# A fused attention, soft MoE and feed-forward kernel: six half-width phases of the feed-forward part, weight conversions over 29 steps

## The chip, the cores and the metric

The kernel runs on one NeuronCore of one Trainium2 chip. The metric is the time of one execution on the device in microseconds (us), as the median of three runs. One further execution was profiled; every row below is from it. The engines are TensorE (PE; its weight loads are PEld), VectorE (DVE), ScalarE (ACT), GpSimd (POOL) and the queue of SyncE (SP), which issues the DMAs.

## The reference, cut to what matters

Three parts follow each other: band attention with global tokens, a soft mixture of experts, and a feed-forward layer. The change is in the last.

```python
def _moe_ref(x, phi, w1, w2):          # x: 2176 tokens of 512
    ...
    return (c @ slot_out).astype(np.float32)      # c: tokens x 32 slots, slot_out: 32 x 512

def _moe2_ref(x, w_in, w_out):         # w_in 512 x 2048, w_out 2048 x 512
    h = x @ w_in
    g = h - np.tanh(h)
    return (g @ w_out).astype(np.float32)
```

The weights w_in and w_out come as 64-bit floats.

## The kernel before

The tokens stand in 17 tiles of 128. Since x is c @ slot_out, h is c @ M with M = slot_out @ w_in, which has 32 rows. M is built in five blocks of columns (`m_rows`, `m_rows_out`, `m_parts`, `m_hi`, `m_lo`; lines 1064 to 1086); blocks 0 to 2 hold the first half of d_ff and are made ahead of the steps, blocks 3 and 4 (512 columns each) during them.

The feed-forward part is a written-out pipeline of 48 steps. The engines take their instructions in the order of the code. A step is a group of 5 or 6 token tiles and one chunk `fc` of 128 of the 2048 columns of d_ff. `PHASES` lists (first tile, number of tiles, first chunk, end): the tiles of a phase accumulate in banks a0 to a5 over its chunks, and two further banks of PSUM, called h, are shared by all else. For each step and each half ("part") of its tiles:

- `g_head` (line 1114, PE): h = M-chunk times c, into an h bank;
- `g_square` (line 1121, ACT): u = h squared;
- `g_tail0`, `g_tail1` (lines 1127 and 1131, DVE): h = (u - 2.5) h, then g = u h. After the second the h bank is free;
- `g_hi` (line 1138, ACT) and `g_lo` (line 1142, POOL): g is split into two rounded parts;
- `ff` (lines 1155 to 1157, PE): three matmuls of 128 x 512 for each tile, high by high, high by low, low by high.

Iteration i of the loop runs the tails of step i + 2, the matmuls of step i, and the heads of steps i + 2 (second part) and i + 3 (first part). So per part the order on PE is nine matmuls (or six) and one head.

Each 128-row chunk of w_out, and each 128 x 512 piece of w_in, is a raw 64-bit array that must be turned into 32-bit floats: one operation on ACT (`f32_head`, line 516) and four on DVE (`clamp`, `shift`, `high`, `low`; lines 521, 524, 529 and 534), the latter put between the tails; a chunk of w_out then gets a high copy on ACT (line 1017) and a low part on POOL (line 1018). `JOBS` says in which step a chunk is converted: numbers under 16 are chunks of w_out, from 24 on pieces of w_in (24 to 27 for M block 3, 28 to 31 for block 4, `MB` says when these are built). Before, steps 1 to 21 convert one each. `LATE` is the order in which the raw arrays are loaded (16 stands for the next piece of w_in), and `AHEAD` how far ahead of its step a load is issued; a raw array lies in a slot that an earlier one gave back.

At the end of a phase `keep_part` (line 1164, ACT) copies a tile's half sum into SBUF, or `emit_out` writes the tile out: the accumulator is scaled, a kept half sum added (on DVE for even tiles of the phase; on ACT and then POOL for odd ones), and a DMA stores it. From iteration 26 on `flag_step` reduces M on DVE (line 1202) to a flag that says whether the short series for tanh was good enough; a branch at the end reads it.

Of the kernel before, what the change touches and what calls it, by code (L numbers as in the profile page):

```python
# [12 lines left out]
ALU = mybir.AluOpType  # L13
# [22 lines left out]

LATE = [0, 1, 2, 3, 4, 5, 6, 7, 16, 16, 16, 16, 8, 16, 16, 16, 16, 9, 10, 11, 12, 13, 14, 15]
FIRST, LASTW = 1, 4  # L40
EARLY, AHEAD = 8, 12


JOBS = {k + 1: c for k, c in enumerate([3, 4, 5, 6, 7, 24, 25, 26, 27, 8, 28, 29, 30, 31, 9, 10, 11, 12, 13, 14, 15])}
MB = {12: 3, 16: 4}

PHASES = [(0, 6, 0, 8), (6, 6, 0, 16), (0, 6, 8, 16), (12, 5, 0, 16)]
THRESH = 0.025


# [8 lines left out]
def band_attention_soft_moe_tanhshrink_kernel(  # L59
# [432 lines left out]
    cool = []  # L492
# [92 lines left out]
    def two_rows():  # L585
        if pairs:
            return pairs.pop(0)
        t = slot()[0]
        return [t[:, 0:512], t[:, 512:1024]]
# [34 lines left out]
    with tc.manual_schedule():  # L624
# [470 lines left out]
        gs_r = [[slot(True)[0][:, 0:768].bitcast(F32R) for _ in range(2)] for _ in range(3)]  # L1095
        n_u = 0
        steps = [(t0, nt, fc, fc == a, fc == b - 1) for t0, nt, a, b in PHASES for fc in range(a, b)]
        u_t, acc_t, part_t = {}, {}, {}

        def parts(i):  # L1100
            return (2 if steps[i][1] > 4 else 1) if i < len(steps) else 0
# [55 lines left out]
                T.matmul(acc_t[j], lhsT=glo[:, c], rhs=whi[fc], start=False, stop=last)  # L1157

        def keep_part(t0, j, scale):
            if not part_t:  # L1160
                for _ in range(3):
                    for t in two_rows():
                        part_t[len(part_t)] = t
            S.activation(out=part_t[t0 + j], in_=acc_t[j], func=AF.Copy, scale=scale)  # L1164

        def emit_out(t0, j, scale, last=False):
# [3 lines left out]
            def scaled(e, c):  # L1170
                if e is V:
                    V.tensor_scalar(out=o[:, c], in0=acc_t[j][:, c], scalar1=scale, scalar2=None, op0=ALU.mult)
                else:
                    S.activation(out=o[:, c], in_=acc_t[j][:, c], func=AF.Copy, scale=scale)
# [2 lines left out]
            r0 = 544 * (i // 4) + 32 + 128 * (i % 4)  # L1177
            if last:
                o2 = fp.tile([128, 512], F32, tag="o", name="o", bufs=6)
                for e, q, c in ((S, S, slice(0, 256)), (V, DMA, slice(256, 512))):  # L1180
                    scaled(e, c)
                    q.dma_start(out=out[r0:r0 + 128, c], in_=o[:, c])
                    o = o2
                return
# [121 lines left out]
        es_x.close()  # L1306
        fp = ctx.enter_context(tc.tile_pool(name="ffn", bufs=2, side="left"))
        for i, (t0, nt, fc, first, last) in enumerate(steps):
            while late and len(free) + len(cool) > 1 and len(LATE) - len(late) < i + AHEAD:
                load_late()  # L1310
            if i == 0:
                continue
# [4 lines left out]
            for part, tiles in enumerate((order[:half], order[half:])):  # L1317
# [6 lines left out]
                        f()  # L1324
                blk = MB.get(i)
                if blk and part == 0:
                    ff(i, tiles[:1])
                    m_rows(blk, None)
                    ff(i, tiles[1:])
                    m_rows_out(blk)  # L1330
                elif blk:
                    ff(i, tiles[:1])
                    m_parts(blk, None)
                    ff(i, tiles[1:])
                    m_hi(blk)
                    m_lo(blk)
                elif i < len(steps) - 3:
                    ff(i, tiles)
                elif i == len(steps) - 1:

                    if part == 0:
                        for k in (3, 2, 1):
                            for j in tiles:
                                ff(len(steps) - k, [j])
                                if k == 1:
                                    emit_out(t0, j, -2.0 / 15.0)
                    else:
                        for j in tiles:
                            for k in (3, 2, 1):
                                ff(len(steps) - k, [j])  # L1350
                            emit_out(t0, j, -2.0 / 15.0, j == tiles[-1])
# [128 lines left out]
```

## Time and profile before

| | |
|---|---|
| three runs, median | 424.33 us (423.94 to 424.89) |
| profiled execution | 426.14 us, with a span of 424.1 us |
| PE busy | 391.2 us (92%) |
| DVE busy | 287.5 us (68%) |
| ACT busy | 216.5 us (51%) |
| POOL busy | 176.6 us (42%) |

The span runs from the first to the last instruction; what the profiled execution took beyond it lies around the kernel. The busy shares are means over stages with different limits, and a busy PE is not PE at its peak, since matmuls overlap in its pipeline. The feed-forward steps fill roughly the second half of the span.

### The profile page before, as it was taken

What the parts mean: (1) busy time and instruction counts of PE and PEld (TensorE: products, weight loads), DVE (VectorE), ACT (ScalarE), POOL (GpSimd) and SP (SyncE); (2) the same over time, 40 slices, a digit from 0 to 9 for tenths busy, and PEclk for the clock granted to TensorE, in tenths of its full rate; (3) what the DMA queues carried; (4) which work ended last, traced back from release to release, by engine and by line L of the source; (5) the groups of instructions that cost most, each with busy time, mean ns of one, the idle gap of its engine ahead of it and who ended that gap; (6) DMA issues with size and microseconds to landing.
All of it is one profiled execution on the core that took longest, in us unless ns stands there. A gap on an engine that the chain in (4) does not pass through costs nothing.

```text
span 424.1 us, 10225 instructions
## 1 busy us (share of the span) xinstructions
PE 391.2 (92%) x3767; PEld 281.3 (66%) x3767; DVE 287.5 (68%) x861; ACT 216.5 (51%) x533; POOL 176.6 (42%) x210
## 2 busy tenths in 40 slices
PE   7798898887988899999999898989999999999994
PEld 4576676675866533325866674767668888888883
DVE  4477597675556626538999897999996567655541
ACT  3567575764856401337655754455555444444441
POOL 5244233432442100015866444345665345744440
PEclk9999899999999989999999998999999999999999
DMA  6999999999989889999440110000004000300003
GB/s 168 269 333 260 322 268 269 305 272 292 297 221 293 277 272 399 418 419 418 179 148 2 51 49 2 0 0 2 1 0 151 0 0 28 123 2 0 0 3 130
DMA packets 33433, 70.42 MB, mean 166 GB/s; under 512 B 4448, under 2 KB 15200, under 8 KB 33376
## 3 DMA queue, kind: packets, MB, share of 16 engines
q1 hardware_dynamic: 33232, 69.56, 51.8%
q8 instruction: 32, 0.52, 0.6%
q14 instruction: 25, 0.20, 0.2%
q10 hardware_dynamic: 144, 0.13, 0.1%
HBM read 65.22 MB, written 4.46 MB: 164 GB/s over the span
## 4 chain that ended last, share of the span: by engine, by line
PE 47%; DMA 17%; DVE 14%; issue 11%; ACT 5%; SPq 3%; POOL 1%; POOLq 0%; DVEq 0%; ACTq 0%
PE a L1157 8%; PE a L1156 8%; PE a L1155 8%; DMA k<-in_k_dram 8%; DVE h L1127 4%; DVE slot L1131 4%; PE sc L236 4%; PE a L952 4%; SPq L100 3%; DMA v_w<-in_w_out_dram 3%; DVE k_w L524 2%; DMA slot<-in_w_in_dram 2%; PE h L1114 2%; PE X L269 2%; PE a L991 2%
## 5 line engine op out<-in xcount | busy, mean ns | idle before, releaser
L1142 POOL TENSOR_TENSOR slot<-slot 128x384 fp32r<-128x384 f32 x96 | 96.6, 1007 | 97.4 <-ACT slot L1138 96.9
L1155 PE MATMUL a<-slot 128*128 128x512 f32 x272 | 108.0, 397 | 1.1 <-ACT q L1164 1.1
L1156 PE MATMUL a<-slot 128*128 128x512 f32 x272 | 108.1, 398 | 0.1
L1157 PE MATMUL a<-slot 128*128 128x512 f32 x272 | 107.9, 397 | 0.0
L1127 DVE SCALAR_TENSOR_TENSOR h<-slot,h 128x384 f32<-128x384 f32 x96 | 51.6, 537 | 40.4 <-ACT slot L1121 39.8
L1138 ACT CAST slot<-slot 128x384 fp32r<-128x384 f32 x96 | 47.6, 496 | 59.0 <-DVE slot L1131 58.9
L1121 ACT ACTIVATE slot<-h 128x384 f32<-128x384 f32 x96 | 45.0, 472 | 42.9 <-PE h L1114 42.3
L1155 PEld LDWEIGHTS a<-slot 128*128 128x128 f32 x272 | 51.3, 189 | 15.7 <-issue 3.0
L1156 PEld LDWEIGHTS a<-slot 128*128 128x128 f32 x272 | 51.3, 188 | 11.6 <-POOL slot L1018 3.0
L1157 PEld LDWEIGHTS a<-slot 128*128 128x128 f32 x272 | 51.2, 188 | 11.0
L201 POOL TENSOR_SCALAR v<-v 32x1300 f32<-32x1300 f32 (+5 forms) x40 | 34.1, 853 | 51.9 <-PE xgp L463 39.3
L246 ACT ACTIVATE sm<-sm,mb 128x128 f32<-128x128 f32 x128 | 41.6, 396 | 25.0 <-DVE mb L242 24.8
L1131 DVE TENSOR_TENSOR slot<-slot,h 128x384 f32<-128x384 f32 x96 | 50.6, 527 | 5.1
L236 PE MATMUL sc<-k,q 128*64 128x128 f32 x512 | 41.3, 303 | 8.2 <-DMA q<-in_q_dram 5.6
L236 PEld LDWEIGHTS sc<-k,q 128*64 128x64 f32 x512 | 34.7, 209 | 14.3 <-issue 8.6
L242 DVE CUSTOM_DVE_ANT_0 sm<-sc,mask 128x128 f32<-128x128 f32 x128 | 30.4, 285 | 10.7 <-PE sc L236 10.2
L1018 POOL TENSOR_TENSOR slot<-k_w,slot 128x512 fp32r<-128x512 f32 x16 | 22.9, 1431 | 32.3 <-DMA v_w<-in_w_out_dram 25.2
L1114 PE MATMUL h<-slot 128*128 128x384 f32 x96 | 33.6, 352 | 1.5 <-DVE slot L1131 0.6
L1114 PEld LDWEIGHTS h<-slot 128*128 128x128 f32 x96 | 17.9, 187 | 14.7 <-DVE slot L1131 10.7
L269 PE MATMUL X<-v,pt 128*32 128x65 f32 x1024 | 22.3, 226 | 0.9 <-issue 0.8
L257 PE MATMUL ptp<-ident,sm 128*128 128x128 f32 x128 | 21.5, 292 | 1.5 <-ACT xT L303 1.4
L269 PEld LDWEIGHTS X<-v,pt 128*32 128x32 f32 x1024 | 16.7, 111 | 6.8 <-issue 5.8
(234 smaller groups left out, 511.4 us busy)
## 6 DMA issues: line engine op xcount, KB each, us to landing
slot<-in_w_dram SPq DMA_DIRECT2D x55, 512.0 KB, 7.5
slot<-in_w_in_dram SPq DMA_DIRECT2D x16, 512.0 KB, 7.1
slot<-in_w_out_dram SPq DMA_DIRECT2D x9, 512.0 KB, 9.8
q<-in_q_dram SPq DMA_DIRECT2D x64, 64.0 KB, 6.2
k<-in_k_dram SPq DMA_DIRECT2D x7, 576.0 KB, 7.9
out_dram<-o SPq DMA_DIRECT2D x15, 256.0 KB, 3.5
v<-in_v_dram SPq DMA_DIRECT2D x8, 390.0 KB, 7.1
v<-in_v_dram SPq DMA_DIRECT2D x8, 195.0 KB, 5.4
```

The source lines that it names most:

```text
L236: T.matmul(sc[64 * i:64 * i + 64, a, :], lhsT=q_b[g % 3][:, 256 * i + jj:256 * i + 256:4], rhs=k[:, i, :, WINDOWS[t][jj][0]], skip_group_c ...
L246: S.activation(out=sm[:, jj, :], in_=sm[:, jj, :], func=AF.Exp, scale=-1.0, bias=mb[:, jj:jj + 1])
L269: T.matmul(X[32 * jj:32 * jj + 32, h, :], lhsT=pt[:, 128 * jj + 32 * h:128 * jj + 32 * h + 32], rhs=v[:, WINDOWS[t][jj][0], 65 * h:65 * h ...
L1114: T.matmul(h, lhsT=mst(128 * fc, 128), rhs=cst(128 * t0 + c.start, n))
L1121: S.activation(out=u, in_=h, func=AF.Square)
L1127: V.scalar_tensor_tensor(out=h, in0=u, scalar=-2.5, in1=h, op0=ALU.add, op1=ALU.mult)
L1131: V.tensor_tensor(out=g, in0=u, in1=h, op=ALU.mult)
L1138: S.copy(out=ghi, in_=g)
L1142: G.tensor_tensor(out=glo, in0=g, in1=ghi.bitcast(F32), op=ALU.subtract)
L1155: T.matmul(acc_t[j], lhsT=ghi[:, c], rhs=whi[fc], start=first, stop=False)
L1156: T.matmul(acc_t[j], lhsT=ghi[:, c], rhs=wlo[fc], start=False, stop=False)
L1157: T.matmul(acc_t[j], lhsT=glo[:, c], rhs=whi[fc], start=False, stop=last)
```

## The change

All 17 tiles go through the first eight chunks of d_ff, in three phases, and then all through the last eight. So 17 half sums are kept instead of 6, in rooms that are taken two at a time as they are needed, and 17 tiles are written out with an addition instead of 6. The 21 conversions stand in steps 1 to 29, mostly two in three steps, the pieces of w_in ahead of the late chunks of w_out. M blocks 3 and 4 are built in steps 13 and 19, behind the matmuls of a part and not between them. Raw arrays are loaded five steps ahead. The last tile, which now has a kept half, is added in two pieces on DVE.

```diff
-LATE = [0, 1, 2, 3, 4, 5, 6, 7, 16, 16, 16, 16, 8, 16, 16, 16, 16, 9, 10, 11, 12, 13, 14, 15]
+LATE = [0, 1, 2, 3, 4, 5, 6, 7, *[16] * 8, 8, 9, 10, 11, 12, 13, 14, 15]
-EARLY, AHEAD = 8, 12
-JOBS = {k + 1: c for k, c in enumerate([3, 4, 5, 6, 7, 24, 25, 26, 27, 8, 28, 29, 30, 31, 9, 10, 11, 12, 13, 14, 15])}
-MB = {12: 3, 16: 4}
-PHASES = [(0, 6, 0, 8), (6, 6, 0, 16), (0, 6, 8, 16), (12, 5, 0, 16)]
+EARLY, AHEAD = 8, 5
+JOBS = {
+    1: 3, 2: 4, 3: 5, 4: 6, 5: 7, 7: 24, 8: 25, 10: 26, 11: 27, 13: 28, 14: 29, 16: 30, 17: 31,
+    19: 8, 20: 9, 22: 10, 23: 11, 25: 12, 26: 13, 28: 14, 29: 15,
+}
+MB = {13: 3, 19: 4}
+PHASES = [(0, 6, 0, 8), (6, 6, 0, 8), (12, 5, 0, 8), (0, 6, 8, 16), (6, 6, 8, 16), (12, 5, 8, 16)]
...
         def keep_part(t0, j, scale):
-            if not part_t:
-                for _ in range(3):
-                    for t in two_rows():
-                        part_t[len(part_t)] = t
+            if not room:
+                room.extend(two_rows())
+            part_t[t0 + j] = room.pop(0)
             S.activation(out=part_t[t0 + j], in_=acc_t[j], func=AF.Copy, scale=scale)
...
+                p = part_t.pop(i, None)
                 for e, q, c in ((S, S, slice(0, 256)), (V, DMA, slice(256, 512))):
-                    scaled(e, c)
+                    if p is None:
+                        scaled(e, c)
+                    else:
+                        V.scalar_tensor_tensor(
+                            out=o[:, c], in0=acc_t[j][:, c], scalar=scale, in1=p[:, c], op0=ALU.mult, op1=ALU.add
+                        )
                     q.dma_start(out=out[r0:r0 + 128, c], in_=o[:, c])
...
-            while late and len(free) + len(cool) > 1 and len(LATE) - len(late) < i + AHEAD:
+            while late and len(free) + len(cool) > 1 and len(LATE) - len(late) < 3 + sum(k < i + AHEAD for k in JOBS):
                 load_late()
...
                 if blk and part == 0:
-                    ff(i, tiles[:1])
+                    ff(i, tiles)
                     m_rows(blk, None)
-                    ff(i, tiles[1:])
                     m_rows_out(blk)
                 elif blk:
-                    ff(i, tiles[:1])
+                    ff(i, tiles)
                     m_parts(blk, None)
-                    ff(i, tiles[1:])
                     m_hi(blk)
                     m_lo(blk)
+                    if blk == 4:
+                        pairs.extend(win[d:d + 2] for d in range(8, 16, 2))
```

On DVE, around step 8: L1130 and L1134 are the tails, L524 to L537 the four conversion operations (their line numbers before were 1127, 1131 and 521 to 534). In the order before, steps 7 and 8 read:

```order
L1127 SCALAR_TENSOR_TENSOR h<-slot,h 128x384
L521 TENSOR_SCALAR pg<-pg 128x512
L1131 TENSOR_TENSOR slot<-slot,h 128x384
L524 TENSOR_SCALAR pg<-pg 128x512
L1127 SCALAR_TENSOR_TENSOR h<-slot,h 128x384
L529 SCALAR_TENSOR_TENSOR pg<-slot,pg 128x512
L1131 TENSOR_TENSOR slot<-slot,h 128x384
L534 SCALAR_TENSOR_TENSOR pg<-slot,pg 128x512
L1127 SCALAR_TENSOR_TENSOR h<-slot,h 128x384
L521 TENSOR_SCALAR k_w<-k_w 128x512
L1131 TENSOR_TENSOR slot<-slot,h 128x384
L524 TENSOR_SCALAR k_w<-k_w 128x512
```

And now, steps 8 (its end) to 10:

```order
L1130 SCALAR_TENSOR_TENSOR h<-slot,h 128x384
L532 SCALAR_TENSOR_TENSOR pg<-slot,pg 128x512
L1134 TENSOR_TENSOR slot<-slot,h 128x384
L537 SCALAR_TENSOR_TENSOR pg<-slot,pg 128x512
L1130 SCALAR_TENSOR_TENSOR h<-slot,h 128x384
L1134 TENSOR_TENSOR slot<-slot,h 128x384
L1130 SCALAR_TENSOR_TENSOR h<-slot,h 128x384
L1134 TENSOR_TENSOR slot<-slot,h 128x384
L1130 SCALAR_TENSOR_TENSOR h<-slot,h 128x384
L524 TENSOR_SCALAR k_w<-k_w 128x512
L1134 TENSOR_TENSOR slot<-slot,h 128x384
L527 TENSOR_SCALAR k_w<-k_w 128x512
```

What moved: before, every pair of tails has conversion operations between and behind; now four tails in a row stand alone in step 9, and the next conversion begins in step 10.

On PE, the product for M block 3 (`h<-q,mask` and the next three; mask holds the slots' outputs by then, q, pg, k_w and v_w the converted pieces of w_in; a_... are the banks of the tiles). In the order before, in step 12:

```order
L1114 MATMUL h<-slot 128x384
L1155 MATMUL a_3617<-slot 128x512
L1156 MATMUL a_3617<-slot 128x512
L1157 MATMUL a_3617<-slot 128x512
L1064 MATMUL h<-q,mask_93 32x512
L1064 MATMUL h<-pg,mask_93 32x512
L1064 MATMUL h<-k_w,mask_93 32x512
L1064 MATMUL h<-v_w,mask_93 32x512
L1155 MATMUL a_3621<-slot 128x512
L1156 MATMUL a_3621<-slot 128x512
L1157 MATMUL a_3621<-slot 128x512
```

And now, in step 13:

```order
L1160 MATMUL a_3604<-slot 128x512
L1158 MATMUL a_3608<-slot 128x512
L1159 MATMUL a_3608<-slot 128x512
L1160 MATMUL a_3608<-slot 128x512
L1067 MATMUL h<-q,mask_93 32x512
L1067 MATMUL h<-pg,mask_93 32x512
L1067 MATMUL h<-k_w,mask_93 32x512
L1067 MATMUL h<-v_w,mask_93 32x512
L1117 MATMUL h<-slot 128x384
L1158 MATMUL a_3621<-slot 128x512
L1159 MATMUL a_3621<-slot 128x512
```

What moved: the product stood behind the first tile's three matmuls, and stands now behind all nine, directly ahead of the next head.

On ACT, the boundary behind step 15, where no tile was kept before. L1141 is g's high copy (1138 before), L519 a conversion's first operation, L1166 the copy of a kept tile, L1124 the square:

```order
L1141 CAST slot<-slot 128x384
L519 ACTIVATE v_w<-slot 128x512
L1166 ACTIVATE k_w<-a_3600 128x512
L1166 ACTIVATE k_w<-a_3604 128x512
L1166 ACTIVATE slot<-a_3608 128x512
L1141 CAST slot<-slot 128x256
L1124 ACTIVATE slot<-h 128x384
L1166 ACTIVATE slot<-a_3621 128x512
L1166 ACTIVATE slot<-a_3625 128x512
L1166 ACTIVATE slot<-a_3629 128x512
L1124 ACTIVATE slot<-h 128x256
```

Three copies stand there ahead of the second part's high copy and of the next step's square, and three behind them.

## Rows read from the trace of the kernel before

**Rows 1.** Windows: PE, PEld, DVE, ACT, POOL busy (count), clock, DMA.

```profile
220.00:230.00 10.00, 9.85 (x39) 6.88 (x40) 9.26 (x17) 5.57 (x12) 6.71 (x6) 1.00 0.05 21
...
330.00:340.00 10.00, 10.00 (x45) 8.20 (x44) 5.90 (x11) 3.98 (x9) 4.70 (x5) 1.00 0.00 0
```

**Rows 2.** Timeline of PE: start us, us, instruction.

```profile
200.60 0.34 PE L1114 MATMUL h<-slot 128*128 128x384 f32 x1
...
219.28 0.44 PE L1114 MATMUL h<-slot 128*128 128x384 f32 x1
...
331.19 0.33 PE L1114 MATMUL h<-slot 128*128 128x384 f32 x1
...
335.72 0.33 PE L1114 MATMUL h<-slot 128*128 128x384 f32 x1
...
364.26 0.28 PE L1114 MATMUL h<-slot 128*128 128x256 f32 x1
...
368.04 0.28 PE L1114 MATMUL h<-slot 128*128 128x256 f32 x1
...
418.02 0.39 PE L1157 MATMUL a<-slot 128*128 128x512 f32 x1
```

**Rows 3.** Timeline of DVE: two conversion steps, first and twelfth start.

```profile
201.87 0.56 DVE L1127 SCALAR_TENSOR_TENSOR h<-slot,h 128x384 f32<-128x384 f32 x1
...
217.81 0.56 DVE L1127 SCALAR_TENSOR_TENSOR h<-slot,h 128x384 f32<-128x384 f32 x1 [0.37 <-ACT slot L1121]
...
218.69 0.54 DVE L1131 TENSOR_TENSOR slot<-slot,h 128x384 f32<-128x384 f32 x1
...
219.15 1.04 DVE L524 TENSOR_SCALAR k_w<-k_w 128x512 int32<-128x512 int32 x1
...
220.58 1.05 DVE L529 SCALAR_TENSOR_TENSOR k_w<-slot,k_w 128x512 int32<-128x512 int32 x1
...
259.23 0.56 DVE L1127 SCALAR_TENSOR_TENSOR h<-slot,h 128x384 f32<-128x384 f32 x1 [0.37 <-ACT slot L1121]
```

**Rows 4.** Timeline of DVE: first step without conversion; an undisturbed start.

```profile
315.92 0.56 DVE L1127 SCALAR_TENSOR_TENSOR h<-slot,h 128x384 f32<-128x384 f32 x1 [0.37 <-ACT slot L1121]
...
319.24 0.56 DVE L1127 SCALAR_TENSOR_TENSOR h<-slot,h 128x384 f32<-128x384 f32 x1 [0.97 <-ACT slot L1121]
...
332.14 0.56 DVE L1127 SCALAR_TENSOR_TENSOR h<-slot,h 128x384 f32<-128x384 f32 x1 [1.04 <-ACT slot L1121]
```

**Rows 5.** Timeline of PE: its three longest waits, a product of M.

```profile
236.64 0.50 PE L1155 MATMUL a<-slot 128*128 128x512 f32 x1 [1.14 <-ACT q L1164]
...
258.31 1.03 PE L1064 MATMUL h<-q,mask 128*32 128x512 f32 x1 [1.69 <-DVE slot L1131]
...
281.73 1.07 PE L1064 MATMUL h<-slot,mask 128*32 128x512 f32 x8 [1.17 <-DVE slot L1131]
...
285.11 1.02 PE L1078 MATMUL h<-ms,mask 128*128 128x512 f32 x2
```

**Rows 6.** Timeline of ACT: two kept tiles.

```profile
236.02 0.57 ACT L1164 ACTIVATE q<-a 128x512 f32<-128x512 f32 x1
...
236.49 0.58 ACT L1164 ACTIVATE k_w<-a 128x512 f32<-128x512 f32 x1
```

**Rows 7.** Timeline of DVE: low half of M; one flag reduction.

```profile
288.23 0.69 DVE L1086 TENSOR_TENSOR slot<-h,slot 64x512 fp32r<-64x512 f32 x1
...
335.54 0.68 DVE L1202 TENSOR_REDUCE phi<-slot 128x1 f32<-128x512 f32 x1
```

**Rows 8.** Timeline of DVE: a conversion ahead of the steps.

```profile
189.45 0.43 DVE L524 TENSOR_SCALAR k_w<-k_w 128x512 int32<-128x512 int32 x1
...
189.92 0.69 DVE L529 SCALAR_TENSOR_TENSOR k_w<-v_w,k_w 128x512 int32<-128x512 int32 x1
```

**Rows 9.** DMA issues from 195 to 320 us: median time to landing.

```profile
slot<-in_w_out_dram SPq DMA_DIRECT2D x4, 512.0 KB, 4.2
```

**Rows 10.** Timeline of DVE: the last output tile's second half.

```profile
418.86 0.42 DVE L1172 TENSOR_SCALAR o<-a 128x256 f32<-128x256 f32 x1 [3.80 <-ACT o L1174]
```

More of the change, by code (lines that the diff above doesn't have):

```diff
@@ L1097, in band_attention_soft_moe_tanhshrink_kernel @@
         steps = [(t0, nt, fc, fc == a, fc == b - 1) for t0, nt, a, b in PHASES for fc in range(a, b)]
-        u_t, acc_t, part_t = {}, {}, {}
+        u_t, acc_t, part_t, room = {}, {}, {}, []
         def parts(i):
```

## The prediction

> **What bounds the kernel now.** I read the windows of the last 225 us first. They hold the 48 steps of the feed-forward part, and two kinds of stretch alternate there: at 220 to 230 VectorE is busy for 9.26 of 10 us and TensorE issues 39 matmuls, at 330 to 340 VectorE is busy for 5.90 and TensorE issues 45 [rows 1]. "Busy" for TensorE is 9.85 and 10.00, since pipelined matmuls overlap, so the counts tell, not the shares. Next I read the heads (the h matmuls) in TensorE's timeline, which cut it into steps. Undisturbed, a step of six tiles lasts 335.72 - 331.19 = 4.53 us, and one of five tiles 368.04 - 364.26 = 3.78 [rows 2].
>
> From these a floor follows. Step 1 starts at 200.60 [rows 2]. Then come 31 steps of six tiles (140.4), 16 of five (60.5), two late products of M with two matmul groups each (2 x (1.07 + 1.02) = 4.2 [rows 5]), 0.2 for the flag's transpose and its neighbours, less about 0.7 because the last two steps have no heads (an estimate, 4 x 0.18). That ends at 405.2. The last matmul really ends at 418.02 + 0.39 = 418.4 [rows 2]. So TensorE loses 13.2 us, and the change can give back no more than that, since it keeps 31 steps of six and 16 of five.
>
> VectorE's timeline shows where they go. In a step with a conversion it does four operations for g (L1127, L1131, twice) and four for the chunk (L521, L524, L529, L534). Eleven such iterations take 259.23 - 201.87 = 57.36 us, 5.21 each [rows 3], against TensorE's 4.53: VectorE falls back 0.68 a step. There are 21 conversions in a row, in steps 1 to 21. How far back it may fall is set by the two h banks: a head waits until L1131 has read the head two before it. At 218.69 + 0.54 = 219.23 L1131 ends, at 219.28 the head starts [rows 2, 3]; this is 1.42 after the iteration's start at 217.81. Once the lag is used up, each step costs TensorE 5.2.
>
> **The change part by part.** The work is nearly unchanged; its place moves. Call D the time at which VectorE starts an iteration, P the time at which TensorE ends the step. D moves on by 5.2 with a conversion. Without one it moves on by 319.24 - 315.92 = 3.32 [rows 4], the only free step right behind conversions in this trace. With five tiles I take 4.85 and 2.95, an estimate: half of the tails and one copy on ScalarE are narrower by a third (0.3 and 0.1 off). The low half of M adds 0.69, a flag reduction 0.68 [rows 7]. D is not before P + 0.95 (332.14 in rows 4 behind 331.19 in rows 2), and P is not before D + 1.42 (1.22 without a conversion).
>
> Steps 1 to 5 convert as before, so steps 4 and 5 lose 0.56 and 0.74 again. Step 6 is now free of a conversion and loses 0.45. From there two conversions and a free step cost VectorE 2 x 5.2 + 3.32 = 13.7, and TensorE 3 x 4.53 = 13.6: level, so the lag stays between 1.6 and 3.4 and up to step 15 nothing more is lost to heads. With five tiles it is 2 x 4.85 + 2.95 = 12.65 against 11.3, so steps 16 to 23 fall back again, helped by 2.1 of TensorE work for M in step 19. Carried through by hand, the lag reaches 3.4 in step 18 (0.8 lost) and 3.2 in step 23 (0.8). Steps 25, 26, 28 and 29 convert, and the flag's reductions, which stood behind all conversions, now start in step 26 beside them: 0.4 lost in step 27, 1.05 in step 29, 1.2 in step 30. From step 31 on nothing is converted, and VectorE catches up.
>
> The M products: before, TensorE stood 1.69 and 1.17 us ahead of them for an h bank, because they came three matmuls into a half step [rows 5]. Behind all nine matmuls the bank has been read for more than 1 us by my times, so I cost the move at 2.1 each, the work alone. If VectorE were 1.2 us later there, the waits would be back.
>
> The kept tiles: 17 instead of 6, three boundaries in place of one, ScalarE copying at 236.49 - 236.02 = 0.47 each [rows 6]. At the old boundary TensorE waited 1.14 for the first copy [rows 5], which stands behind a copy that waits for VectorE. I take 0.6 after step 7 and 0.9 after step 23, where the lag is 2.1 and 3.2, and nothing after step 15, where copies start 1.3 us earlier; there ScalarE passes on about 1 us to VectorE, which is in the lags above. Bounds: nothing, or 1.14 at each of three, 3.4. The boundaries after steps 31 and 39 have the form of one in the old trace that shows no wait; I take 0.2. Low halves of late chunks cost 0.6 in all (0 to 1.5). The last tile now has both halves added on VectorE, one after the other. The second half already waited for ScalarE's first (idle 3.80, released by that instruction [rows 10]), so the end costs nothing, at most 0.4.
>
> The sum of losses is 0.56 + 0.74 + 0.45 + 0.8 + 0.8 + 0.4 + 1.05 + 1.2 + 0.6 + 0.9 + 0.2 + 0.6 = 8.3, against 13.2: a gain of 4.9. The profiled execution took 426.14 with a span of 424.1, so 2.0 lie around it; it would become 421.2. It lies 1.8 above the median of the runs, 424.33, which becomes 419.4.
>
> One price is open: a conversion costs more here than by itself. L524 takes 1.04 and L529 1.05 in the stretch, but 0.43 and 0.69 ahead of it, when GpSimd has nothing to do [rows 3, 8]. The Trainium skill (SBUF — State Buffer, section "Who interferes with whom") says that VectorE and GpSimd share a pair of ports as an exclusive lock, taken by VectorE operations with two SBUF inputs or in a two-port mode, and that the second to come blocks fully. By that rule a spread schedule in which the two no longer meet would have conversions at their short prices and nearly all of the 13.2 us back; the rows alone say only that the long prices are there whenever g's low parts run beside them, and those stay.
>
> **The rivals.** The first is that larger gain: with 0.61 and 0.36 less per conversion, VectorE needs 4.24 a step, less than TensorE's 4.53, and only the boundaries (about 1.5) and the start stay: a gain near 11, 413. For it: the short prices exist. Against: every step, also a free one, still has its two GpSimd subtractions. A half of it, with the lag gone in some steps, gives 415 to 417.
>
> The second: ScalarE's copies of kept tiles hold both banks and VectorE. Each of three boundaries then costs the old wait, 1.14, and the 1 us passed on to VectorE, because g's square stands behind the copies: 6.4 where I count 1.5 and 1, so 3.9 of the gain go, 423.3. For it: the old wait. Against: VectorE was at its full lag then, and has room after step 15.
>
> The third ends slower: raw chunks come late. They are loaded five steps ahead instead of up to twelve, and several wait for the slot of an earlier chunk. ScalarE's first operation on a chunk stands three steps behind the issue, 11.3 us with five tiles. Behind it on ScalarE wait the squares and the high copies, for these VectorE, GpSimd and TensorE. Landing took 4.2 us there [rows 9]. It decides against the change from a sum of lateness of 4.9 us, say two chunks that land 14 us after their issue (2 x 2.7). Three such chunks give 427.5.
>
> The fourth: nothing comes of it, since a free step does not recover. That needs 3.9 instead of 3.32 in the eight free steps (8 x 0.6 = 4.9); I have a single row for it. It gives 424.
>
> **How the numbers follow.** The forecast (a gain of 3 to 7, 417.3 to 421.3) has 0.61; the larger gain 0.14 (411.5 to 417.3); the copies 0.12 (421.3 to 423.4); no change 0.06; late chunks 0.07. A measurement of this kernel tells 0.2% from no change, 0.85 us. Faster is 0.87, the first three; same 0.06; slower 0.07. The range for 8 in 10 takes the forecast, the copies and the upper half of the larger gain: 415.5 to 423.0.
>
> **What would show it.** In the changed trace, free steps (6, 9, 12) should last about 3.3 us on VectorE when it is behind, and heads should come every 4.53 us from step 9 to 15, with the two M products at about 1 us each and no wait ahead of them. Losses should sit in steps 4 to 6, 18, 23 and 27 to 30, where VectorE stays above nine tenths. The waits for kept tiles should be under 1 us. The last matmul should end near 413.5. I am wrong if ScalarE waits for a DMA in steps 7 to 29, if TensorE waits over 1 us for L1166 at more than one boundary, or if L524 and L529 shrink to their short prices in most conversions.

## The result, and the profile after

| | before | after |
|---|---|---|
| runs, median | 424.13 us (422.01 to 424.89) | 418.40 us (417.19 to 419.62) |
| profiled execution | 426.14 us, span 424.1 | 419.62 us, span 417.8 |
| start of step 1 to end of the last matmul | 217.81 us | 210.79 us |

The ratio of the times is 0.9873, with an interval of 0.9826 to 0.992: the kernel is faster by 5.7 us in the medians, where 4.9 was forecast.

The third row of the table is called the stretch below. It leaves out what lies ahead of the steps, and that is needed: step 1 starts anywhere between 197.4 and 205.2 us in the profiled executions of this study, ahead of all that was changed. The prediction's floor for the stretch is 405.2 - 200.6 = 204.6. What is above it is loss: 13.2 before, 6.2 after, a gain of 7.0 where the sum had 4.9. Each stretch is that of one profiled execution. Some executions are slow as a whole: ratios with intervals leave them out and medians don't, and of the profiled ones two are slow (the copies first at all boundaries, and M behind in the kernel before), but their steps without a wait last the same 4.53 us.

The windows of the kernel after, in the columns of [rows 1]; the middle one is a stretch in which two steps in three convert:

```profile
220.00:230.00 10.00, 9.86 (x39) 6.82 (x39) 9.16 (x15) 5.33 (x11) 6.72 (x7) 1.00 0.22 60
250.00:260.00 10.00, 10.00 (x46) 8.20 (x45) 8.08 (x16) 5.26 (x11) 4.56 (x5) 1.00 0.19 54
330.00:340.00 10.00, 10.00 (x46) 8.15 (x45) 10.00 (x18) 5.00 (x11) 5.35 (x6) 1.00 0.00 0
```

From 220 to 230 all is as it was. From 250 to 260 TensorE issues 46 matmuls, although VectorE converts. From 330 to 340 VectorE is busy for all of the 10 us, with conversions and flag reductions, and TensorE still issues 46.

The timeline of PE after, which answers to [rows 2, 5]:

```profile
201.35 0.34 PE L1117 MATMUL h<-slot 128*128 128x384 f32 x1
...
246.94 0.33 PE L1117 MATMUL h<-slot 128*128 128x384 f32 x1
...
251.48 0.33 PE L1117 MATMUL h<-slot 128*128 128x384 f32 x1
...
265.31 0.44 PE L1117 MATMUL h<-slot 128*128 128x384 f32 x1 [0.29 <-DVE slot L1134]
...
307.70 0.45 PE L1117 MATMUL h<-slot 128*128 128x384 f32 x1 [0.49 <-DVE slot L1134]
308.74 0.50 PE L1158 MATMUL a<-slot 128*128 128x512 f32 x1 [0.60 <-ACT q L1166]
...
311.96 0.50 PE L1158 MATMUL a<-slot 128*128 128x512 f32 x1 [0.70 <-ACT v_w L1166]
...
411.75 0.39 PE L1160 MATMUL a<-slot 128*128 128x512 f32 x1
```

A step in the middle lasts 251.48 - 246.94 = 4.54 us, undisturbed. Of the waits for M's products one of 0.29 is left. At the boundary behind step 23 TensorE waits for two copies of kept tiles. The last matmul ends at 412.14, and the span goes on for 5.66 us behind it (before, 424.1 - 418.41 = 5.69): the new end costs nothing.

The losses by step, from the heads as in the prediction (above 4.53 us, or 3.78 with five tiles; steps under 0.1 are left out; a step with M products has about 2.1 of work in it that belongs to the floor):

| step | 4 | 5 | 6 | 7 | 8 | 11 | 12 | 13 | 16 | 19 | 20 | 21 | 22 | 23 | 24 | 31 | 36 |
|---|---|---|---|---|---|---|---|---|---|---|---|---|---|---|---|---|---|
| before | .56 | .74 | .73 | .72 | 1.72 | .53 | 5.82 M | | 3.59 M | .31 | .72 | .73 | .67 | .25 | | | .21 |
| after | .60 | .72 | .68 | .27 | .32 | | | 2.50 M | | 2.01 M | .41 | | .12 | .66 | 1.88 | .22 | .12 |

In step 12 of the kernel before a second thing is at work, which the prediction did not see. The windows of the kernel before, at the M product's wait of 1.69 us [rows 5] and behind it (the last three numbers are the granted clock, the DMA share and GB/s):

```profile
256.00:258.00 2.00, 0.62 (x3) 0.19 (x1) 2.00 (x4) 0.56 (x1) 1.25 (x2) 1.00 0.00 0
260.00:262.00 2.00, 2.00 (x9) 1.51 (x6) 0.97 (x3) 0.59 (x1) 0.00 (x0) 0.55 0.00 0
```

Directly behind that wait the granted clock of TensorE falls to half (1.2 GHz instead of 2.4) from 258.39 to 261.80. That is at most 1.7 us of the 5.82 lost there. In the kernel after, the clock stands at 1.00 from step 1 to the last matmul.

The timeline of DVE after: starts of iterations, and reductions for the flag (L1210).

```profile
229.08 0.56 DVE L1130 SCALAR_TENSOR_TENSOR h<-slot,h 128x384 f32<-128x384 f32 x1 [0.37 <-ACT slot L1124]
...
232.41 0.56 DVE L1130 SCALAR_TENSOR_TENSOR h<-slot,h 128x384 f32<-128x384 f32 x1 [0.97 <-ACT slot L1124]
...
237.45 0.56 DVE L1130 SCALAR_TENSOR_TENSOR h<-slot,h 128x384 f32<-128x384 f32 x1 [0.37 <-ACT slot L1124]
...
276.01 0.56 DVE L1130 SCALAR_TENSOR_TENSOR h<-slot,h 128x384 f32<-128x384 f32 x1 [2.16 <-ACT slot L1124]
...
280.12 0.55 DVE L1130 SCALAR_TENSOR_TENSOR h<-slot,h 128x384 f32<-128x384 f32 x1
...
293.12 0.56 DVE L1130 SCALAR_TENSOR_TENSOR h<-slot,h 128x384 f32<-128x384 f32 x1
...
298.08 0.55 DVE L1130 SCALAR_TENSOR_TENSOR h<-slot,h 128x384 f32<-128x384 f32 x1
...
329.50 0.56 DVE L1130 SCALAR_TENSOR_TENSOR h<-slot,h 128x384 f32<-128x384 f32 x1 [0.38 <-ACT slot L1124]
...
334.10 0.67 DVE L1210 TENSOR_REDUCE phi<-slot 128x1 f32<-128x512 f32 x1
334.69 0.55 DVE L1130 SCALAR_TENSOR_TENSOR h<-slot,h 128x384 f32<-128x384 f32 x1
```

An iteration's tiles here are those of the step two ahead, whose tails it does. A free one lasts 3.33 us (229.08 to 232.41), as forecast; the one of step 9 lasts 3.68, with a wait for GpSimd. A conversion of w_in lasts 5.04 with six tiles (232.41 to 237.45) and 4.11 with five (276.01 to 280.12), one of w_out 4.96 with five (293.12 to 298.08, step 20, directly behind another conversion of w_out); I had taken 4.85 for either with five tiles. The iterations of steps 22 and 23 already do tails of six tiles and last 5.11 and 5.22, against steps of 3.78. An iteration with a conversion and a flag reduction lasts 5.19 (329.50 to 334.69) to 5.41 (step 26), not 5.9: behind the reduction the next tail doesn't wait, while without one it waits 0.37 for ScalarE's square.

### The profile page after: what moved, and what is told of

Same layout as the page of the kernel before. It is cut to its first block, busy times and chain, and to the rows that moved or that the text cites. A ratio compares the mean times of both kernels' runs of the same rounds, so it can differ in the third digit from the quotient of the medians.

```text
span 417.8 us, 10253 instructions
## 1 busy us (share of the span) xinstructions
PE 386.5 (93%) x3767; PEld 282.2 (68%) x3767; DVE 285.2 (68%) x864; ACT 219.5 (53%) x541; POOL 185.7 (44%) x214
## 4 chain that ended last, share of the span: by engine, by line
PE 62%; DMA 16%; DVE 8%; issue 6%; SPq 3%; ACT 2%; POOL 1%; DVEq 0%; POOLq 0%
PE a L1159 12%; PE a L1160 12%; PE a L1158 12%; DMA k<-in_k_dram 7%; DMA slot<-in_w_dram 6%; PE a L955 4%; PE a L994 4%; SPq L103 3%; PE h L1117 3%; PE sc L239 3%; DVE h L1130 2%; DVE slot L1134 2%; PE X L272 2%; DMA v<-in_v_dram 2%; DMA q<-in_q_dram 2%
## 5 line engine op out<-in xcount | busy, mean ns | idle before, releaser
L1145 POOL TENSOR_TENSOR slot<-slot 128x384 fp32r<-128x384 f32 x96 | 99.7, 1043 | 82.8 <-ACT slot L1141 78.7
L1130 DVE SCALAR_TENSOR_TENSOR h<-slot,h 128x384 f32<-128x384 f32 x96 | 51.5, 536 | 36.4 <-ACT slot L1124 36.0
L1141 ACT CAST slot<-slot 128x384 fp32r<-128x384 f32 x96 | 47.7, 497 | 52.9 <-DVE slot L1134 52.5
L1124 ACT ACTIVATE slot<-h 128x384 f32<-128x384 f32 x96 | 45.3, 473 | 32.9 <-PE h L1117 32.4
L1134 DVE TENSOR_TENSOR slot<-slot,h 128x384 f32<-128x384 f32 x96 | 50.6, 527 | 5.8 <-DVE h L1130 0.5
L1021 POOL TENSOR_TENSOR slot<-k_w,slot 128x512 fp32r<-128x512 f32 x16 | 22.2, 1391 | 32.3 <-ACT slot L1020 32.2
```

The source lines that it names most:

```text
L1124: S.activation(out=u, in_=h, func=AF.Square)
L1130: V.scalar_tensor_tensor(out=h, in0=u, scalar=-2.5, in1=h, op0=ALU.add, op1=ALU.mult)
L1134: V.tensor_tensor(out=g, in0=u, in1=h, op=ALU.mult)
L1141: S.copy(out=ghi, in_=g)
L1145: G.tensor_tensor(out=glo, in0=g, in1=ghi.bitcast(F32), op=ALU.subtract)
```

## The experiments

The theory is the prediction's: VectorE's lag in conversion steps holds the h banks, and free steps between them let it recover. Each run below has the stretch of its profiled execution beside its time.

**Only the spread taken back.** The new phases, with 17 kept tiles, and the conversions packed in steps 1 to 21:

```diff
-JOBS = { 1: 3, ... 5: 7, 7: 24, 8: 25, 10: 26, ... 29: 15 }
+JOBS = {k + 1: c for k, c in enumerate([3, 4, 5, 6, 7, *range(24, 32), *range(8, 16)])}
```

> The changed kernel with its 21 conversions packed into steps 1 to 21 again, one per step, in the new order of chunks; phases, kept tiles and M products stay as changed. Theory A (VectorE's lag is what costs; a conversion iteration is long against a step of six tiles, about 5.1 against 4.53, but in steps of five tiles it is 4.1 against 3.78 as the changed trace has it): the free steps give back little that packing would lose, since the boundary behind step 23 and steps 25 to 30 then have no conversions. Losses of 5 to 5.5 us where the changed kernel has 6.2: 417.5 to 418.5 us, the same within 0.9. Theory B (spreading is what brings the gain): packing gives back most of it, 421.5 to 424 us.

Measured: 425.68 us, ratio to before 1.0039 (1.0004 to 1.0073), and a stretch of 217.81, that of the kernel before. Theory B is right, and even its range was too low. So the spread brings all of the 7.0 us; the clock does not fall in this run's steps, so they do not rest on that. The rest of the change brings nothing on balance, within the 1.7 us that half clock may have cost before. That the phases make the spread possible is read from the code, not shown: by the old ones chunk 8 is needed from step 16 on, by the new ones from step 24, and no run spreads in the old phases. The number that I had for theory A was too low because I took 4.1 us for every conversion with five tiles. Here one of w_out behind another of w_out lasts 4.99, by the timeline of DVE of this run (the lines are numbered as before the change, L524 is `shift`, L529 `high`):

```profile
287.19 0.55 DVE L1127 SCALAR_TENSOR_TENSOR h<-slot,h 128x384 f32<-128x384 f32 x1
...
288.53 1.04 DVE L524 TENSOR_SCALAR k_w<-k_w 128x512 int32<-128x512 int32 x1
...
289.82 1.17 DVE L529 SCALAR_TENSOR_TENSOR k_w<-slot,k_w 128x512 int32<-128x512 int32 x1
...
292.18 0.56 DVE L1127 SCALAR_TENSOR_TENSOR h<-slot,h 128x384 f32<-128x384 f32 x1 [0.26 <-ACT slot L1121]
```

**M's place**, in the changed kernel (back behind the first tile's matmuls) and in the one before (behind all of a part's):

```diff
-                    ff(i, tiles)
+                    ff(i, tiles[:1])
                     m_rows(blk, None)
+                    ff(i, tiles[1:])
```

> The changed kernel with the products for M blocks 3 and 4 put back behind the first tile of a part. Theory A: with VectorE only 1.6 us behind in steps 13 and 19 the h bank is free by the time that TensorE comes, so at most 0.5 us each is lost: 418.4 to 419.4. Theory C (the place of the M products is worth their old waits, 1.69 and 1.17, and the VectorE idle time behind them): 420.5 to 422 us.

Measured: 417.29 us, ratio 0.9836 (0.9782 to 0.989), stretch 210.30, theory A's side.

> The kernel before with the products for M blocks 3 and 4 behind all matmuls of a part, as the change puts them, and nothing else changed. The stretch took 217.8 us. With VectorE 3.6 us behind in those steps the bank is still late behind nine matmuls, by about 0.8 in place of 1.7, and VectorE idles less: 215.5 to 217, that is 1 to 2 us of the time. If the place of the products is worth nothing, 217.6 to 218.2; if it were a large part of the change's 7.0, under 215.

Measured: 424.37 us, ratio 1.0005 (0.997 to 1.0039), stretch 217.77. M's new place gains nothing in either kernel (in the changed one the old place is 0.5 us shorter). In the one before, step 12 still loses 5.09 (with the clock at half from 264.05 to 267.46) and step 16 3.79, with waits for VectorE of 0.34 at the first product and of 1.31 and 1.30 at the heads behind the two: the waits of 1.69 and 1.17 [rows 5] were VectorE's lag, which shows at the next instruction that needs a bank, wherever that stands. What the prediction put down to the move (the waits gone) came from the spread.

**The flags behind the conversions:**

```diff
-            flag_step(i - 26)
+            flag_step(i - 32)
```

> The changed kernel with the flag's reductions started in step 32 and not 26, so that none stands beside a conversion. My prediction's sum has 2.65 us lost to them in steps 27 to 30: it expects 415.8. The changed trace has these steps at 4.53 us, with the reductions in the time in which VectorE waited for ScalarE: it expects no difference, 418.0 to 418.6.

Measured: 422.09 us, ratio 0.9899 (0.9836 to 0.9963), stretch 210.69 against 210.79. The time lies above both forecasts, but step 1 began at 205.15 in the profiled execution, 3.8 us later than in that of the changed kernel; the stretch decides. The flags cost nothing where they are; the 2.65 us of the sum were wrong. Iterations with a conversion and a reduction last 0.04 to 0.15 us longer than the same ones without the reduction here (5.41, 5.19 and 5.32 against 5.26, 5.05 and 5.28).

**The last conversion ahead of the boundary moved behind it:**

```diff
-    19: 8, 20: 9, 22: 10, 23: 11, 25: 12, 26: 13, 28: 14, 29: 15,
+    19: 8, 20: 9, 22: 10, 24: 11, 25: 12, 26: 13, 28: 14, 29: 15,
```

> The changed kernel with the conversion of step 23 moved to step 24, so that the last step ahead of a boundary with kept tiles has none. Theory A (the waits for kept tiles are VectorE's lag handed on by ScalarE, whose copies stand behind the high copies of g): of the 2.5 us lost in steps 23 and 24 under 1 stays, 416.5 to 417.2. Theory D (the copies themselves, 0.47 us each and six in series, hold the banks): steps 23 and 24 lose as before, 418.2 to 418.8.

Measured: 420.0 us, ratio 0.9883 (0.9832 to 0.9933), stretch 211.21. Steps 23 and 24 together lose 2.01 of 2.54, where theory A had under 1 and theory D all; step 27 loses a new 0.67. By itself this decides nothing, because the moved conversion puts its ScalarE operation (L519, 0.67) ahead of the first three copies. The timeline of PE of this run has the only wait for a copy:

```profile
312.21 0.50 PE L1158 MATMUL a<-slot 128*128 128x512 f32 x1 [1.16 <-ACT q L1166]
```

It is 1.16 instead of 0.60, about as much longer as L519 lasts, and the second wait, 0.70, is gone.

**The copies of kept tiles ahead of g's high copies**, at all three boundaries:

```diff
+                if last and fc != 15:
+                    for j in tiles:
+                        keep_part(t0, j, -2.0 / 15.0)
                 if part < parts(i + 2):
...
```

> The changed kernel with ScalarE's copies of kept tiles put ahead of the high copies of g in the last step of a phase, not behind them. From step 1's start to the last matmul the changed kernel took 210.8 us. Theory A (the waits of 0.60 and 0.70 us for kept tiles in step 24 are VectorE's lag, handed on by ScalarE's order): they go, step 24 lasts under 5.2 us in place of 6.4, and the stretch 209.3 to 209.8. Theory D (the copies themselves hold the banks): step 24 lasts 6 us or more, the stretch 210.5 to 211.

Measured: 421.14 us, ratio 0.9868 (0.9781 to 0.9954), stretch 211.63. Step 24 loses 0.28 instead of 1.88, as theory A has it, but its stretch (209.3 to 209.8) does not come: steps 9, 16 and 17 lose 0.66, 0.81 and 0.27, which were free, and some later ones up to 0.15. At those boundaries the squares and high copies now stand behind the copies. The timeline of ACT after, at the boundary behind step 23, shows what the order does:

```profile
307.68 0.51 ACT L1141 CAST slot<-slot 128x384 fp32r<-128x384 f32 x1 [0.58 <-DVE slot L1134]
308.10 0.59 ACT L1166 ACTIVATE q<-a 128x512 f32<-128x512 f32 x1
...
310.51 0.52 ACT L1141 CAST slot<-slot 128x384 fp32r<-128x384 f32 x1 [0.84 <-DVE slot L1134]
310.93 0.48 ACT L1124 ACTIVATE slot<-h 128x384 f32<-128x384 f32 x1
311.31 0.59 ACT L1166 ACTIVATE v_w<-a 128x512 f32<-128x512 f32 x1
```

ScalarE waits 0.58 and 0.84 for VectorE's tail with the high copy, and the copies, whose banks are ready, stand behind it. TensorE's waits of 0.60 and 0.70 for them (308.74 and 311.96 above) follow.

**VectorE without conversions:** the four VectorE operations are left out in steps 1 to 29, so that the weights there are not converted, and the flag is forced to the branch that is normally taken.

> The changed kernel without VectorE's four conversion operations in the steps (ScalarE's, GpSimd's and the loads stay); the late weights are therefore not converted, and the flag is forced. Theory A (all losses but M's own work come from VectorE's lag): the stretch takes 205 to 206, near the floor of 204.6, and steps 8, 16 and 24 lose under 0.5 each to kept tiles. Theory D (kept tiles cost by themselves): steps 8, 16 and 24 lose 0.6 to 1.9 as in the changed kernel, the stretch takes 207 to 208.5.

Measured: 412.11 us, ratio 0.9747 (0.9684 to 0.9809), stretch 204.74 against the floor of 204.6. So all of the loss but 0.1 us goes with VectorE's conversion operations. Step 24 loses 0.25 with all of its copies in place: behind a high copy, they cost much only where there is a lag. The run before shows the other half: with the lag there and the copies first, step 24 loses as little.

**GpSimd without the low parts** of g and of the chunks (two of each three matmuls take other operands of the same shape; all three are then high by high, so the product of the high parts is added three times and the output is not the right one):

> The changed kernel without GpSimd's two subtractions (g's low part and the low part of a chunk of w_out in the steps); TensorE uses the high parts in their place, so the number of matmuls is the same and the low parts are left out of the result. If the long prices of L527 and L532 (1.04 and 1.05 to 1.5) come from GpSimd working beside them, they fall to 0.43 and 0.69, a conversion iteration lasts 4.2 to 4.5 us, steps 4 to 6 lose nothing where they lost 2.0, and the stretch takes 205.5 to 207. If they have another cause, steps 4 to 6 lose 0.6 to 0.7 each as before and the stretch takes 210 to 211.

Measured: 415.14 us, ratio 0.9765 (0.9678 to 0.9853), stretch 205.09. Steps 4 to 6 lose nothing; step 24 keeps 0.56. First the timeline of DVE in this run, one iteration with a conversion of w_out (L527 is `shift`, L532 `high`):

```profile
218.10 0.56 DVE L1130 SCALAR_TENSOR_TENSOR h<-slot,h 128x384 f32<-128x384 f32 x1 [0.37 <-ACT slot L1124]
...
219.38 0.42 DVE L527 TENSOR_SCALAR k_w<-k_w 128x512 int32<-128x512 int32 x1
...
220.52 0.68 DVE L532 SCALAR_TENSOR_TENSOR k_w<-slot,k_w 128x512 int32<-128x512 int32 x1
...
222.64 0.56 DVE L1130 SCALAR_TENSOR_TENSOR h<-slot,h 128x384 f32<-128x384 f32 x1 [0.37 <-ACT slot L1124]
```

It lasts 4.54 us, a step of TensorE, and the two operations take 0.42 and 0.68. In the changed kernel, with GpSimd's subtractions (L1021 for a chunk, L1145 for g), the timelines of POOL and DVE:

```profile
219.20 1.47 POOL L1021 TENSOR_TENSOR slot<-k_w,slot 128x512 fp32r<-128x512 f32 x1
219.45 0.54 DVE L1134 TENSOR_TENSOR slot<-slot,h 128x384 f32<-128x384 f32 x1
219.91 1.05 DVE L527 TENSOR_SCALAR k_w<-k_w 128x512 int32<-128x512 int32 x1
...
234.45 1.02 POOL L1145 TENSOR_TENSOR slot<-slot 128x384 fp32r<-128x384 f32 x1 [1.37 <-ACT slot L1141]
234.54 1.47 DVE L532 SCALAR_TENSOR_TENSOR q<-slot,q 128x512 int32<-128x512 int32 x1
235.94 0.54 DVE L1134 TENSOR_TENSOR slot<-slot,h 128x384 f32<-128x384 f32 x1
...
293.41 1.29 POOL L1021 TENSOR_TENSOR slot<-k_w,slot 128x512 fp32r<-128x512 f32 x1 [0.16 <-ACT slot L1020]
293.71 1.28 DVE L524 TENSOR_SCALAR k_w<-k_w 128x512 f32<-128x512 f32 x1
```

L527 begins at 219.91 inside of a subtraction that ends at 220.67, and ends 0.29 behind it; L532 begins 0.09 behind the start of one that ends at 235.47, and ends 0.54 behind it. In both cases the operation does most of its work after GpSimd's end. The tail at 219.45, whose h comes from PSUM, lies wholly inside of the subtraction and takes its usual 0.54. That is what the Trainium skill (SBUF — State Buffer, section "Who interferes with whom") says of an exclusive lock for VectorE operations with two SBUF inputs or in a two-port mode; the trace agrees for the most part, with 0.42 against 1.05 and 0.68 against 1.47, of which all but 0.13 and 0.14 of the usual time lies behind GpSimd's end. What gives VectorE its lag is this meeting; its operations by themselves fit into a step.

The low part of a chunk (L1021) runs on GpSimd one step behind the chunk's conversion. At 293.41 it is that of the chunk of step 19, and it stretches the `clamp` (L524) of step 20 to 1.28. So a conversion of w_out costs the step behind it: L527 takes 1.03 to 1.07 in the eight steps (1 to 5, 23, 26, 29) in which such a low part runs beside it, and 0.41 or 0.42 in the other 13.

**Order against the lock.** If meetings cost so much, another order in a step could avoid them:

```diff
-                    for f in ops[2 * part:2 * part + 1]:
-                        f()
+                    if part == 0:
+                        for f in ops[0:1]:
+                            f()
                     g_tail1(i + 2, part)
-                    for f in ops[2 * part + 1:2 * part + 2]:
+                    for f in ops[1:2] if part == 0 else ops[2:4]:
                         f()
```

> The changed kernel with one edit: in the second half of a step both tails of g stand ahead of the third and fourth conversion operation (tail 0, tail 1, high, low in place of tail 0, high, tail 1, low). Theory A: the losses of the changed kernel are VectorE's lag, and a part of an iteration of about 5.0 us is order: the wait of 0.37 for ScalarE's square ahead of the first tail, and the h bank held behind the high operation. With the tails first the square of the next step runs beside high and low, the bank is free about 1.2 us earlier, and an iteration takes 4.2 to 4.7 us. The stretch from the start of step 1 to the last matmul falls from 210.8 to 206 to 208 us, the device time to 414 to 416; steps 4 to 6 lose under 0.3 each. Theory B: the length of VectorE's work decides (GpSimd's subtractions beside it), not its order; the iteration stays at 4.9 or more, the stretch within 1 us of 210.8.

Measured: 425.03 us, ratio 0.9994 (0.9952 to 1.0035), stretch 216.46. Both theories fell: the order matters, and this one is 5.7 us worse. The timelines of POOL and DVE of this run:

```profile
217.48 0.55 DVE L1130 SCALAR_TENSOR_TENSOR h<-slot,h 128x384 f32<-128x384 f32 x1
...
220.90 0.69 DVE L532 SCALAR_TENSOR_TENSOR k_w<-slot,k_w 128x512 int32<-128x512 int32 x1
...
221.61 1.03 POOL L1145 TENSOR_TENSOR slot<-slot 128x384 fp32r<-128x384 f32 x1 [0.87 <-ACT slot L1141]
221.62 1.56 DVE L537 SCALAR_TENSOR_TENSOR k_w<-slot,k_w 128x512 int32<-128x512 int32 x1
...
223.10 0.55 DVE L1130 SCALAR_TENSOR_TENSOR h<-slot,h 128x384 f32<-128x384 f32 x1
```

L532 is short now, but g's low part starts 0.01 us ahead of L537, which takes 1.56 instead of 0.68; the iteration lasts 5.62 instead of 5.25. The meeting has moved and grown.

> The kernel before with the same edit of the second half of a step and nothing of the change. Theory A (order inside the step is worth as much as the spread): an iteration falls below TensorE's 4.53 us, so that even 21 conversions in a row lose nothing, and the stretch falls from 217.8 to 207 to 212 us, as low as the change itself brings it (210.8). Theory B (VectorE needs more than a step whatever the order, so only a spread helps): the iteration stays above 4.8 us, the stretch at 214 us or more.

Measured: 426.32 us, ratio 1.0003 (0.9965 to 1.0042), stretch 217.68: theory B's side. Each packed step loses 1.1 instead of 0.7, and steps 12 and 16 give it back (3.43 and 2.70 instead of 5.82 and 3.59). The earlier tail may free the bank earlier there, which is argued; in step 12 up to 1.7 us of the difference is the clock, which does not fall in this run's steps.

> The changed kernel with the tails first, and the copies of kept tiles put ahead of ScalarE's high copies at one boundary only, that behind step 23, where the changed kernel loses 1.88 us. If step 24's loss is copies that stand behind a high copy which waits for VectorE, and the lag is still there with the tails first, this takes up to 1.3 us more than the tails first alone. If the lag is gone with the tails first, it is worth nothing (within 0.4 us in the stretch), or costs up to 0.7 in steps 24 and 25, as the same order did in steps 9 and 16 of the run with all three boundaries.

Measured: 425.76 us, ratio 1.0029 (0.999 to 1.0067), stretch 216.82; step 24 loses 1.67 (1.30 with the tails first alone). The copies' order gains nothing here. The timelines of POOL, DVE and PE of this run show why:

```profile
313.45 1.02 POOL L1145 TENSOR_TENSOR slot<-slot 128x384 fp32r<-128x384 f32 x1 [0.97 <-ACT slot L1141]
313.81 1.22 DVE L532 SCALAR_TENSOR_TENSOR k_w<-slot,k_w 128x512 int32<-128x512 int32 x1
...
317.98 0.44 PE L1117 MATMUL h<-slot 128*128 128x384 f32 x1 [1.33 <-DVE slot L1134]
```

TensorE waits for no copy in step 24 any more. But the high copy behind the copies comes later, and with it g's low part on GpSimd, which now meets L532 too (1.22, with the tails first alone 0.69). VectorE's iteration of step 23 lasts 5.98 instead of 5.61, and a head waits 1.33 for it.

**The late chunks in other steps:**

```diff
-    19: 8, 20: 9, 22: 10, 23: 11, 25: 12, 26: 13, 28: 14, 29: 15,
+    18: 8, 20: 9, 22: 10, 25: 11, 26: 12, 27: 13, 28: 14, 29: 15,
```

> The changed kernel with the late chunks of w_out in other steps: 8 in step 18, 9 in 20, 10 in 22, and 11 to 15 in a row in steps 25 to 29 (before the edit 19, 20, 22, 23, 25, 26, 28, 29), nothing else. Theory A: the 1.88 us lost in step 24 are copies of kept tiles that come when VectorE still lags, and the 1.2 in steps 20 to 23 are the lag itself. A w_out conversion with five tiles costs VectorE 4.96 against TensorE's 3.78 (1.2 back), a free step 3.05 (0.7 up); three in place of four, and a free step directly ahead of the boundary, leave step 24 about 1.9 us less lag: it loses 0.4 (what it lost with VectorE free of conversions was 0.25 to 0.41), steps 20 to 23 under 0.6. Five conversions in a row in steps 25 to 29 add 0.68 each to the lag, 3.4 in all, and cost TensorE 0 to 0.6. The stretch goes from 210.8 to 208.5 to 209.5 us, the device time to about 416.5 to 417.5. Theory B: the loss in step 24 is the copies' own (six of them, whatever the lag): it stays above 1.3 us, and the five conversions in a row add 0.6 to 1.5, so that the stretch is 210.5 to 211.5.

Measured: 421.1 us, ratio 0.9817 (0.9759 to 0.9875), stretch 211.74. At the boundary the timeline of PE has half of the waits:

```profile
306.32 0.44 PE L1117 MATMUL h<-slot 128*128 128x384 f32 x1 [0.15 <-DVE slot L1134]
307.36 0.50 PE L1158 MATMUL a<-slot 128*128 128x512 f32 x1 [0.60 <-ACT q L1166]
```

Step 24 loses 0.95 instead of 1.88, the direction of theory A; the stretch is above the ranges of both. Steps 28 to 30 lose 2.15, not 0 to 0.6: the five iterations with conversions in a row last 5.72 (with waits for ScalarE in it), 5.41, 5.33, 5.33 and 5.32, in all 4.5 us more than TensorE's steps, and not 3.4. The flag reductions are little of that: packed conversions of w_out without them last 5.26 in the kernel before. What is won at the boundary is lost five steps on.

The same run corrects the price of w_out. The timeline of DVE, conversions of steps 18 and 20, with five tiles:

```profile
283.08 0.55 DVE L1130 SCALAR_TENSOR_TENSOR h<-slot,h 128x384 f32<-128x384 f32 x1
...
287.13 0.55 DVE L1130 SCALAR_TENSOR_TENSOR h<-slot,h 128x384 f32<-128x384 f32 x1
...
292.41 0.56 DVE L1130 SCALAR_TENSOR_TENSOR h<-slot,h 128x384 f32<-128x384 f32 x1
...
296.51 0.55 DVE L1130 SCALAR_TENSOR_TENSOR h<-slot,h 128x384 f32<-128x384 f32 x1
```

Both convert chunks of w_out and last 4.05 and 4.10, as short as w_in: no low part of an earlier chunk meets them. The 4.96 taken for a w_out conversion with five tiles was one behind another. No version here with the full computation has a shorter stretch than the changed kernel by more than the 0.5 us of M's old place.

## Why the prediction was right

Time, direction and mechanism held; the loss left is 6.2 where the sum had 8.3. That the two are so close is in part luck: terms of 4.65 (flags 2.65, step 18 0.8, low halves 0.6, copies behind step 7 0.6) did not show, and losses of 2.7 were missed (0.8 in steps 6 to 8, 0.4 at M, 0.4 in steps 20 to 23, 1.0 in step 24, 0.1 at the emits). Term by term:

- **The floor** of 204.6 was right: 204.74 without conversions.
- **Steps 4, 5, 6** were forecast at 0.56, 0.74 and 0.45 and lose 0.60, 0.72, 0.68; steps 7 and 8, at nothing (the copies apart), lose 0.27 and 0.32. The lag was at its limit there, and the one free iteration is followed by two conversions.
- **Steps 9 to 15** lose nothing but M's work and 0.4 with it (2.50 and, in step 19, 2.01, against 2.1 each), nearly as forecast. The sign was right, the reason not: the place of M gave nothing (stretch 210.30 and 217.77 in the two runs).
- **Step 18** was to lose 0.8 and loses nothing, since a conversion with five tiles lasts 4.1 us and not 4.85. **Steps 20 to 23** lose 1.19 for 0.8: the conversion of step 20 lasts 4.96, having the low part of the chunk before on GpSimd beside it, and those of steps 22 and 23 already have tails of six tiles (5.11 and 5.22), which the sum took as five.
- **The flags**, 0.4 + 1.05 + 1.2, cost nothing: the largest error of the sum. I added 0.68 to the iteration, but 0.37 of it lies in the time for which the first tail waits for ScalarE, the iteration grows by 0.15 at most, and that lies in the room that the free steps leave.
- **The kept tiles**, 0.6 and 0.9, cost nothing behind step 7 and 1.88 behind step 23. The rival of the copies was right for one boundary of three; its condition was VectorE's lag, shown from three sides: without conversions 0.25, with less lag 0.95 (without GpSimd's low parts 0.56), and, with the lag there, 0.28 with copies ahead of the high copies.
- **Emits** at 0.2 are 0.22 in step 31 and 0.12 in step 36; the **low halves** at 0.6 don't show; the **end** costs nothing, as forecast.

The losses of 13.2 were put down to VectorE's lag alone; at most 1.7 of them, in step 12, was TensorE's clock at half behind a wait that the lag had made.

The rival of the larger gain had its mechanism right and its reason wrong. GpSimd is the cause of the long prices (without it the losses are 0.5 in all), but the spread parts the two only in part: L527 still takes 1.05 where a conversion of w_out stands just ahead, and L532 1.03 to 1.56 with tails of six tiles; with five it is short, and L537 takes 1.18 in its place. The prediction gave g's low parts as the reason for both long prices; that of L527 stands beside the low part of a chunk. Its sign of being wrong, short prices for both in most conversions, did not come: L527 is short in 13 of 21 conversions (9 of 21 before), L532 in 5. The late chunks didn't come: from 225 to 350 us ScalarE waits for no DMA. The free step recovers (3.33, not 3.9), so the fourth falls as well.

Why two conversions in three steps is about the limit can be estimated from rows. In a w_out conversion step VectorE's four operations take 0.42 + 0.42 + 0.68 + 0.68 = 2.2 us without GpSimd, and GpSimd's subtractions 2 x 1.0 + 1.28, which is 5.5 for a step of 4.53 if the two exclude each other. Over two such steps and a free one it is 2 x 5.5 + 2.0 = 13.0 for 13.6. They do not exclude each other wholly, since packed iterations last 5.26 and not 5.5; no run here tried another engine for the chunk's low part, or a free step behind every conversion of w_out.

## What to carry to other kernels

An engine that is free for a third of the time can still be the limit of a stretch: cut the stretch into steps, compare the iteration of each engine with the step, and count how much lag the buffers allow; then spreading the extra work is worth what the lag costs. Here nothing that was done at the place where the wait shows (M's products, the copies) brought more than 0.5 us. Before adding an operation's duration to an iteration, look for the wait that it will lie in; and before reordering operations of VectorE, look at what GpSimd does at that moment, since an order that parts one pair may bring another together. Copies that are ready should not stand behind an operation that waits, but putting them first costs elsewhere when nothing is late.

## What the runs showed of the hardware

- A GpSimd subtraction of 128 x 384 (1.02 us) or 128 x 512 (1.27 to 1.56 us) stretches a VectorE operation on SBUF that meets it from 0.42 to 1.05 or 1.28, or from 0.68 to as much as 1.56 us, and leaves one that reads PSUM at 0.54.
- Directly behind a wait of TensorE of 1.69 us the granted clock was 0.5 (1.2 GHz) for 3.41 us, and matmuls of 0.40 us took 0.63 to 0.79.
- The start of step 1 varies by 7.8 us between the profiled executions, though the code ahead of it is nearly the same in all kernels here. Part of it goes with the granted clock ahead of step 1, whose mean is 0.99 in the two earliest (197.44 and 198.85) and 0.97 in the three latest (204.45 to 205.21), but not all: it is 0.95 with a start at 203.67. That the clock is the cause is not shown. A change of a few us in a later stage is read better from that stage than from the whole time.
